# Two-level first-layer products in the last two groups of a fused attention and Fourier-mix kernel

## The chip, the cores and the metric

The kernel runs on one core of a Trainium2 chip. The core has engines that run side by side, each through its own list of instructions in order: TensorE (PE) multiplies matrices into eight banks of PSUM, VectorE (DVE) does elementwise work, ScalarE (ACT) applies functions and copies, GpSimd (POOL) does elementwise work on SBUF alone, and SyncE (SP) issues DMA transfers. They wait for each other through semaphores. The metric is the device time of one execution in microseconds (us), lower is better; the median of the runs shown is compared.

## The reference

All arrays are float32. There are 8 batches, 8 heads, 576 rows and a head dimension of 64, so that a row has 512 values after the heads are joined.

```python
q_s = softmax of q over its last axis
k_s = softmax of k over the sequence
x   = q_s @ (k_s^T v), heads joined               # (8, 576, 512)
mixed = real(fft over the columns of fft over the rows of x)
u   = x + mixed
un  = (u - mean(u)) / sqrt(var(u) + 1e-6)         # over the last axis
out = u + relu(un @ w_ch1) @ w_ch2                # w_ch1 512 x 2048, w_ch2 2048 x 512
```

## The kernel before, in words

The 8 x 576 rows are worked on as nine groups of 512 rows: eight groups of a batch's own rows, and one, number 8 in the code, that collects the 64 rows left over in every batch ("shared"). The groups run in the order 0 to 6, 8, 7. A group's place in that list is its `order`, so that order 7 is the shared group and order 8 is the last one. Attention, the Fourier mixing and the normalization of the following group run between the matrix products of the current one; in the last two orders only the normalization of the last group is left to run beside them, in the down half of order 7.

The two layers are most of the work. Each is a product of a 2 x 2 block matrix of weights with a 2 x 2 block matrix of activations, done with Winograd's form of Strassen's scheme: seven products (numbered 1 to 7, in the order 1, 6, 5, 7, 2, 4, 3 of `ORDER`) in the place of eight, and some sums of blocks before and after.

The up half (`up`, L1532) makes h = relu(un @ w_ch1). It goes through four quarters j. A quarter takes two pairs of column blocks of w_ch1 (i = 0, 1) and for each of the seven products runs four matmuls of 256 columns, L1544: two row blocks of the contraction for each i. `strassen` (L1499) places the products in three PSUM banks: 1 and then 2 in `ba`, 6, 7 and 4 in `bb`, 5 and 3 in `bc`, each added onto what is there. Between them ACT copies product 1 out (s1, L1515), DVE forms u2 and u3 (L1514) and the four blocks of h (L1555), and ACT applies relu (L1551, L1556). As an example, h22 is u3 plus product 5, and h12 is u2 plus products 5 and 3. At the end of the quarter `a_side` (L405 to L408) makes the four block sums of h that the second layer's products need, on DVE in orders 7 and 8 and on POOL before.

The down half (`deep_down`) makes h @ w_ch2 and adds it to u. There the products are already done at two levels: product 1 is done at one level (L1641), the others are split again into seven products of 128-column matmuls (L1671), two first-level products beside each other as a unit. `a_step` (L1617) makes the sums of h for them, `ends` (L1678 and the copies at L1685 and L1692) takes the results out of the banks, `into` (L1621) and `sums` (L1624) add the results to the rows x of the group, on POOL up to order 6 and on DVE in orders 7 and 8.

The normalization (`norm`) lays the normalized rows out as `unT`, seven blocks of 512 values per partition: four raw ones and the three or four block sums that the first layer needs (L1396, L1400, L1405).

The weights don't fit beside the activations. All block sums of the weights are made once, early on, and written to DRAM: `w1s` for the first layer at one level, `w2s` and `w2d` for the second at one and two levels. A list, `plan`, holds the stream of weight blocks of all orders. Four buffers hold it: when the block n has served its last product, `used(n)` issues the load of block n + 4 on SP's queue. SP issues its transfers in order.

The order of the work is written out by hand: every step has a time in a list, `timed` adds the steps of one order, and the list sorted by these times is recorded; each engine then runs its own instructions in that recorded order. The times have no other meaning. `UP` is the length of an up half in this list and `TWICE` that of a down half.

Of the kernel before, what the change touches and what calls it, by code (L numbers as in the profile page):

```python
# [52 lines left out]
HD = D // 2  # L53
# [66 lines left out]
def at(t, script):  # L120
    return [(t + dt, step) for dt, step in script]
# [17 lines left out]
class _Block:  # L139
    def __init__(self, ctx, tc, q, kT, v, w1, w2, ft, cd, out):  # L140
# [3 lines left out]
        nc = self.nc  # L144
# [6 lines left out]
        c = self.const  # L151
# [30 lines left out]
        nc.gpsimd.memset(self.sign[:], -1.0)  # L182
        nc.gpsimd.memset(self.sign[0:W], 1.0)
        d = self.dram
        self.w1s = [d.tile([P, 7, HD], F32, tag=f"w1s{p}", name=f"w1s{p}", bufs=1) for p in range(NP)]
        self.w2s = d.tile([7, P, NP, HD], F32, tag="w2s", name="w2s", bufs=1)

        self.w2d = d.tile([P, len(DEEP), GT], F32, tag="w2d", name="w2d", bufs=1)
        self.plan, self.base = [], {}
        for at in range(1, B + 1):  # L190
            self.base[at] = len(self.plan)
            self.plan += [self.w1s[p][:].rearrange("p a n -> p (a n)") for pair in PAIRS for p in pair]
# [59 lines left out]
    def flat(self):  # L252
        return self.turned().rearrange("p r n -> p (r n)")
# [163 lines left out]
    def combine(self, layer, p):  # L417

        nc = self.nc
        w = self.w2sb if layer else self.w1sb  # L420

        pairs = lambda a: a.rearrange("p (s n) -> p s n", s=2)
        temp = lambda n: self.work.tile([P, 2, HD], F32, tag=n, name=n, bufs=1)[:]
        if layer == 0 and p < 2:
            t, four = [temp("s1"), temp("u2")] if p == 0 else [temp("u3"), temp("s1")], None
        else:
            a = p // 2 * 2 - 2 + NP * (p % 2) if layer == 0 else NP + 2 * (p % 2)
            four = self.w1sb[:, a:a + 2, :].rearrange("p a n -> p (a n)")
            if layer and p % 4 == 3:
                four = self.spare_words  # L430
            t = [pairs(four[:, i * D:(i + 1) * D]) for i in range(2)]
            if layer and p % 4 == 2:
                t, four = [temp("s1"), temp("u2")], None
        quarter = lambda i: w[:, p + NP * (i // 2), (i % 2) * HD:(i % 2 + 1) * HD]
        place = lambda i: t[i > 4][:, int(i in (4, 6)), :]
        halves = lambda a: a.rearrange("p (s n) -> p s n", s=2)
        if layer == 0:
            ops = ((4, ALU.add, 2, 3), (2, ALU.subtract, 0, 2), (5, ALU.subtract, 4, 0), (6, ALU.subtract, 1, 5))
            engines, times = (nc.vector,) * 4, (0, 0.4, 0.8, 1.2)
            to, first, second = self.w1s[p][:], slice(0, 2), slice(2, 3)  # L440
# [1091 lines left out]
    def up(self, order, g):  # L1532

        nc, V = self.nc, self.nc.vector
        steps = []
        base, e = self.base[order], V if order >= B - 1 else nc.gpsimd
        for j in range(NP // 2):
            hp = lambda i, h=self.hpairs(j, 2): h[:, :, i, :]

# [22 lines left out]
            job = self.strassen(product, 1, {(1, 1): c11, (2, 1): other(1), (2, 2): other(3), (1, 2): other(2)})  # L1562
            t = 2 * len(ORDER) * j
            steps += at(t, job) + [(t + 2 * len(ORDER) - 0.5 + 5 * i * (j < NP // 2 - 1), lambda n=base + 2 * j + i: self.used(n)) for i in range(2)]
        return steps

    def used(self, n):
# [23 lines left out]
    def deep_down(self, g, order):  # L1591
# [24 lines left out]
            to = own(m)  # L1616
            e.tensor_tensor(out=to(o), in0=to(x), in1=to(y), op=op)  # L1617

        def into(u, d, m):
            x = self.xs[g, u][:, :, d * HD:(d + 1) * HD].rearrange("p c (e n) -> p c e n", n=P)  # L1620
            E.tensor_tensor(out=x, in0=x, in1=tile(m), op=ALU.add)  # L1621

# [57 lines left out]
        def ends(unit, n):  # L1680
# [14 lines left out]
            if n == 3:  # L1695
# [1 line left out]

        after = {(2, 4): [(7, into, 1, 0, 4), (9, into, 0, 0, 2)],
                 (7, 6): [(1, sums, 6, 1), (3, into, 0, 1, 6), (5, sums, 7, 6), *(((7, into, 1, 0, 7), (9, into, 1, 1, 7)) if last else ())],
                 (5, 3): [(0.6, into, 1, 1, 5), (1.2, into, 0, 1, 5), (1.8, into, 0, 1, 3)] if last else  # L1700
                         [(4, into, 1, 0, 7), (5.5, into, 1, 1, 7), (7, into, 1, 1, 5), (8.5, into, 0, 1, 5), (10, into, 0, 1, 3)]}
        names = {1: ("bb", "bb"), 2: ("bc", "bb"), 4: ("ba", "bb")}
        n, t = 2 * len(ORDER), 0
# [130 lines left out]
def kernel(ctx: ExitStack, tc: tile.TileContext, q, kT, v, w1, w2, ft,  # L1834
                                                           cd, out):
    blk = _Block(ctx, tc, q, kT, v, w1, w2, ft, cd, out)

    def timed(t, order, g):
        b = order + 1
# [91 lines left out]
    t = 0  # L1931
    for order, g in enumerate(groups[1:], 1):
        later += timed(t, order, g)
        t += UP + (TWICE if order > 1 else UP)
# [59 lines left out]
```

## Time and profile before

| what | value |
|---|---|
| three runs | 1006.04, 1007.01 and 1007.47 us; median 1007.01 us |
| span of the profiled execution | 1006.6 us, the only time shown of that execution; 0.4 us below the median of the runs |
| up half of order 7 | 815.03 to 863.51 us |
| down half of order 7 | 863.51 to 908.37 us |
| up half of order 8 | 908.37 to 956.72 us |
| down half of order 8, to the last product | 956.72 to about 1002.6 us |

The limits of the halves are the starts of PE's matmuls of L1544 and L1641 in the time line. In the time line a row is a start, a length, the engine, the line, the operation, output and inputs, the shape and the number of records; in brackets stand the idle time before it and what ended it. PE's ends are modelled and overlap the next start, so that the pace of PE is read from start to start. A row of the groups view ends with busy time, the mean of one in ns, and the idle time before such instructions. A row of the stretches view has the length, the busy time of PE, PE's weight loads (PEld), DVE, ACT and POOL with their counts, the granted TensorE clock, the busy share of the DMA engines and GB/s. A DMA row has the size of one transfer and the median time from issue to landing.

### The profile page before, as it was taken

How to read it: one execution, taken by the hardware profiler on the slowest of the kernel's cores; microseconds unless marked ns; L12 is line 12 of the kernel's file. 1: busy time of each engine (PE TensorE's matmuls, PEld its weight loads, DVE VectorE, ACT ScalarE, POOL GpSimd, SP SyncE). 2: the span in 40 equal slices, each digit the busy share in tenths (PEclk: the TensorE clock that was granted, in tenths of full speed). 3: DMA queues.
4: the chain of work that ended last, by engine and by line, in shares of the span. 5: the costliest groups of instructions: out<-in, count | busy, mean ns of one | idle time of the engine just before them, and what ended most of it. 6: DMA issues, size and time to landing. Idle time of an engine off the chain costs nothing.

```text
span 1006.6 us, 19808 instructions
## 1 busy us (share of the span) xinstructions
PE 995.6 (99%) x7562; PEld 855.7 (85%) x7562; DVE 718.6 (71%) x1356; ACT 493.2 (49%) x1277; POOL 442.9 (44%) x445
## 2 busy tenths in 40 slices
PE   8999999999999999999999999999999999999998
PEld 6844464888888899889988998899889998998897
DVE  6898898666765887588756877688667945685563
ACT  4585642872468228832775177625772342151200
POOL 4263420357535637664655465655646450040000
PEclk9999999999999999999999999999999999999999
DMA  9987499687989666975677577847753765674573
GB/s 300 258 281 245 158 240 346 205 243 226 342 283 272 230 230 219 266 237 210 251 220 242 206 269 237 253 174 270 231 204 135 267 213 200 224 265 172 183 256 132
DMA packets 123559, 236.37 MB, mean 235 GB/s; under 512 B 24184, under 2 KB 88440, under 8 KB 112840
## 3 DMA queue, kind: packets, MB, share of 16 engines
q1 hardware_dynamic: 123096, 234.58, 71.0%
q8 instruction: 60, 0.98, 0.4%
q14 instruction: 35, 0.29, 0.1%
q10 hardware_dynamic: 288, 0.26, 0.1%
q0 software_dynamic: 80, 0.26, 0.1%
HBM read 199.94 MB, written 39.06 MB: 237 GB/s over the span
## 4 chain that ended last, share of the span: by engine, by line
PE 87%; DVE 7%; ACT 3%; DMA 1%; issue 1%; SPq 0%; POOL 0%; DVEq 0%; POOLq 0%
PE bb L1544 16%; PE ba L1544 11%; PE bc L1544 11%; PE bb L1671 10%; PE ba L1671 7%; PE bc L1671 7%; PE bb L1641 5%; PE bc L1479 2%; PE bb L1760 2%; PE two L840 2%; PE one L755 2%; PE two L1207 1%; PE two L1264 1%; PE ba L1479 1%; PE bc L1760 1%; PE ba L1760 1%
## 5 line engine op out<-in xcount | busy, mean ns | idle before, releaser
L1544 PE MATMUL bb<-unT,big 128*128 128x256 f32 x768 | 183.3, 380 | 0.0
L1544 PEld LDWEIGHTS bb<-unT,big 128*128 128x128 f32 x768 | 144.8, 190 | 20.7 <-DVE u L1514 0.7
L1556 ACT ACTIVATE big<-big 128x512 f32<-128x512 f32 x96 | 59.8, 629 | 147.6 <-DVE big L1555 141.0
L1544 PE MATMUL ba<-unT,big 128*128 128x256 f32 x512 | 123.9, 382 | 0.0
L1544 PE MATMUL bc<-unT,big 128*128 128x256 f32 x512 | 121.5, 380 | 0.1
L817 ACT ACTIVATE qT<-q 32x128 f32<-32x128 f32 x384 | 117.9, 307 | 5.9 <-DVE q L807 0.8
L1544 PEld LDWEIGHTS bc<-unT,big 128*128 128x128 f32 x512 | 96.9, 190 | 13.7 <-DVE big L1555 0.5
L1544 PEld LDWEIGHTS ba<-unT,big 128*128 128x128 f32 x512 | 95.5, 190 | 13.9 <-issue 0.5
L1514 DVE TENSOR_TENSOR u<-bb,s 128x512 f32<-128x512 f32 x66 | 45.2, 685 | 85.0 <-PE bb L1544 66.5
L1671 PE MATMUL bb<-big 128*128 128x128 f32 x848 | 103.8, 276 | 0.2 <-DVE u L1678 0.2
L1671 PEld LDWEIGHTS bb<-big 128*128 128x128 f32 x848 | 98.9, 192 | 1.0 <-DVE u L1678 1.0
L1390 POOL COPY unT<-unT 32x256 f32<-32x256 f32 x98 | 42.0, 428 | 90.2 <-DVE unT L1382 85.9
L1621 POOL TENSOR_TENSOR x<-x,big 128x512 f32<-128x512 f32 x45 | 60.9, 1368 | 46.0 <-DVE big L1678 19.7
L1617 DVE TENSOR_TENSOR big<-big 128x512 f32<-128x512 f32 x98 | 79.9, 842 | 0.0
L1671 PE MATMUL ba<-big 128*128 128x128 f32 x640 | 79.0, 276 | 0.0
L1671 PEld LDWEIGHTS ba<-big 128*128 128x128 f32 x640 | 75.0, 192 | 0.8
L1390 ACT COPY unT<-unT 32x256 f32<-32x256 f32 x126 | 50.7, 402 | 31.3 <-DVE unT L1382 29.5
L804 POOL TENSOR_TENSOR q<-q,qm 128x512 f32<-128x512 f32 x24 | 25.8, 1073 | 88.2 <-DVE qm L799 53.1
L405 POOL TENSOR_TENSOR big<-big 128x512 f32<-128x512 f32 x24 | 30.4, 1268 | 68.4 <-ACT big L1556 68.4
L1641 PE MATMUL bb<-big 128*128 128x256 f32 x256 | 58.3, 379 | 0.0
L1555 DVE TENSOR_TENSOR big<-bc,u 128x512 f32<-128x512 f32 x64 | 44.0, 688 | 17.3 <-PE bc L1544 16.4
L1641 PEld LDWEIGHTS bb<-big 128*128 128x128 f32 x256 | 48.0, 190 | 6.1
(336 smaller groups left out, 1917.9 us busy)
## 6 DMA issues: line engine op xcount, KB each, us to landing
big<-w2d SPq DMA_DIRECT2D x67, 1024.0 KB, 4.6
big<-w1s SPq DMA_DIRECT2D x64, 896.0 KB, 4.7
big<-w2s SPq DMA_DIRECT2D x16, 1024.0 KB, 4.8
big<-in_w_dram SPq DMA_DIRECT2D x21, 512.0 KB, 6.0
w2d<-big SPq DMA_DIRECT2D x42, 256.0 KB, 6.5
kb<-in_kT_dram SPq DMA_DIRECT2D x28, 320.0 KB, 7.8
q<-in_q_dram SPq DMA_DIRECT2D x28, 256.0 KB, 6.0
vt<-in_v_dram SPq DMA_DIRECT2D x84, 80.0 KB, 2.7
```

Source lines behind the costliest of these rows:

```text
L405: e1.tensor_tensor(out=to(4), in0=at(2), in1=at(3), op=ALU.add)
L817: nc.scalar.activation(to[t, i * Q:i * Q + Q], one, ACT.Exp)
L1390: copy(to, of)
L1514: plus = lambda t: V.tensor_tensor(out=temp(t), in0=box["bb"][:], in1=box["s1"][:], op=ALU.add)
L1544: nc.tensor.matmul(bank()[:, i, :], lhsT=w[:, WA_AT[m], k * P:(k + 1) * P], rhs=self.unT[g][:, B_AT[m], k, :], start=first and i == 0 and ...
L1555: steps = [(0, lambda: V.tensor_tensor(out=hp(i), in0=bank()[:], in1=u()[:], op=ALU.add)), (0.8, lambda: nc.scalar.activation(hp(i), hp(i) ...
L1556: (0.8, lambda: nc.scalar.activation(hp(i), hp(i), ACT.Relu))]
L1617: e.tensor_tensor(out=to(o), in0=to(x), in1=to(y), op=op)
L1621: E.tensor_tensor(out=x, in0=x, in1=tile(m), op=ALU.add)
L1641: nc.tensor.matmul(box[name][:, i, :], lhsT=h[p][:, A_AT[m], i * P:(i + 1) * P], rhs=self.stream[n][:, p, :], start=p == 0 and (m != 1 or ...
L1671: nc.tensor.matmul(box[place[n]][:, i, :], lhsT=own(m)(A_AT[n])[:, f, :], rhs=w[:, r // 2, r % 2 * P:r % 2 * P + P], start=first and f == ...
L1760: nc.tensor.matmul(bank()[:, i, :], lhsT=h[p][:, A_AT[m], i * P:(i + 1) * P], rhs=w[:, p, :], start=first and i == 0 and p == 0, stop=p == ...
```

## The change

In orders 7 and 8 the function `wide_up` takes the place of `up`. Products 2 and 4 of order 7, and 2, 3 and 4 of order 8 (`WIDE`), leave the four quarters and are done each for all four quarters at once, at two levels, as a unit of seven products with four 128-column matmuls (`wide_unit`). The units stand behind the first quarter. The quarters keep the products 1, 6, 7, 5 and, in order 7, 3.

- Banks: in a quarter product 7 now has the bank `one` to itself, 1 has `ba`, 6 has `bb`, 5 and 3 share `bc`. In a unit 1 and 2 share `ba`, 6 and 4 use `bb`, 5 and 3 share `bc`, 7 has `one`.
- Results: a unit leaves its product in a slot of h that the a-side sums will fill later (`WIDE_AT`: slots 5, 6 and 4 for products 2, 3 and 4). `more` on POOL joins it with the other parts of h, in the first quarter after the unit, in the later ones ahead of the quarter's own sum where that can be (h12 in order 8) or after it (h21). h11 is a DVE sum of product 1's bank and the slot.
- Sums of h: of the four block sums of a quarter, two stay on DVE and two go to POOL, and all stand in the next quarter's sequence; the last quarter has all four on DVE.
- Operands: the raw weight blocks of products 2, 4 and 3 are loaded once, during the down half of order 6, into buffers that have no further use (`wide_load`: kb; vt, q and qT; F and ft). Their block sums are made by `wide_sums`: product 2's on DVE in the down half of order 6, those of 4 and 3 on POOL in the up half of order 7. The block sums of `unT` for each unit are made on POOL in order 7 and on DVE in order 8, 128x128 each.
- Five `into` steps at the end of order 7's down half go from DVE to POOL.
- The weight stream is the same. The eight DRAM tiles `w1s` become one, `w1c`, with the same contents.

```diff
+SHORT = (1, 6, 7, 5)
+UNIT, WIDE_AT = 7.2, {2: 5, 3: 6, 4: 4}
+WIDE = {B - 1: (2, 4), B: (2, 3, 4)}
...
-        self.w1s = [d.tile([P, 7, HD], F32, tag=f"w1s{p}", name=f"w1s{p}", bufs=1) for p in range(NP)]
+        self.w1c = d.tile([P, NP, 7, HD], F32, tag="w1s", name="w1s", bufs=1)
+        self.w1s = [self.w1c[:, p] for p in range(NP)]
...
-        base, e = self.base[order], V if order >= B - 1 else nc.gpsimd
+        base, e = self.base[order], nc.gpsimd
+        if order >= B - 1:
+            return self.wide_up(order, g)
...
+    def wide_load(self, m):
+        self.wide[m], pairs = self.wide_places(m)
+        for i, t in enumerate(pairs):
+            p = NP // 2 * (1 - i)
+            raw = self.w1c[:, p:p + NP // 2, WA_AT[m], :]
+            if t is not None:
+                self.nc.sync.dma_start(t, raw)
+                continue
+            for k in range(2):
+                self.nc.sync.dma_start(self.wide[m][2 * i + k], raw[:, :, k * P:(k + 1) * P])
...
+    def wide_unit(self, g, m, e, *at_sums):
...
+        place = {1: "ba", 2: "ba", 6: "bb", 4: "bb", 5: "bc", 3: "bc", 7: "one"}
...
+            for j in range(4):
+                nc.tensor.matmul(box[name][:, j, :], lhsT=self.wide[m][A_AT[n]][:, j, :], rhs=b_at(B_AT[n]),
+                                 start=first and j == 0, stop=True, skip_group_check=True)
...
+        def ends(n):
+            if n == 1:
+                nc.scalar.copy(temp("s1"), box["ba"])
+            if n == 6:
+                plus(temp("u2"), "bb", "s1")
+            if n == 7:
+                plus(temp("u3"), "one", "u2")
+                plus(to(3), "bc", "u3")
+            if n == 2:
+                nc.scalar.copy(to(0), box["ba"])
+            if n == 4:
+                plus(to(2), "bb", "u3")
+            if n == 3:
+                plus(to(1), "bc", "u2")
...
+        for k, n in enumerate(ORDER):
+            steps += [(1.02 * k, lambda n=n: product(n)), (1.02 * k + 0.9, lambda n=n: ends(n))]
...
+    def wide_up(self, order, g):
+        base, wide = self.base[order], WIDE[order]
+        products = [m for m in (*SHORT, 3) if m not in wide]
+        size = 2 * len(products)
+        def part(t, j, done):
+            def product(m, i):
+                name = {1: "ba", 6: "bb", 7: "one", 5: "bc", 3: "bc"}[m]
...
+                for k in range(2):
+                    nc.tensor.matmul(box[name][:, i, :], lhsT=w[:, WA_AT[m], k * P:(k + 1) * P], rhs=self.unT[g][:, B_AT[m], k, :],
+                                     start=m != 3 and i == 0 and k == 0, stop=k == 1, skip_group_check=True)
...
+            for k, m in enumerate(products):
+                for i in range(2):
+                    put(2 * k + i, product, m, i)
...
+            put(3.9, lambda: plus(temp("u2"), "bb", own(0) if j == 0 else got("s1")))
+            put(5.9, lambda: plus(temp("u3") if j else hp(1), "one", got("u2")))
+            put(7.9, lambda: plus(hp(3), "bc", got("u3") if j else own(1)))
...
+            if 3 not in wide or j == 0:
+                put(size + 0.7 * (3 in wide) - 0.1, lambda: plus(hp(2), "bc", got("u2")))
+            else:
+                put(4.7, lambda: more(WIDE_AT[3], got("u2"), 3))
+                put(8.7, lambda: plus(hp(2), "bc", own(WIDE_AT[3])))
...
+            put(1.95, lambda: plus(hp(0), "ba", own(WIDE_AT[2])))
+            put(6.7, lambda: more(1, got("u3"), 4))
+            if last:
+                sides(size + 2.6, size + 3.4, True)
+            else:
+                sides(size + (3.95 if 3 in wide else 2.3), size + (8.3 if 3 in wide else 3), False)
...
+        if order == B - 2:
+            steps += [(t + UP + dt, lambda m=m: blk.wide_load(m)) for m, dt in ((2, 4), (4, 12), (3, 25))]
+            steps += at(t + UP, blk.wide_sums(2, blk.nc.vector, 40, 41, 44, 45))
+        if order == B - 1:
+            steps += at(t, blk.wide_sums(4, blk.nc.gpsimd, 10.5, 10.6, 10.7, 10.8) + blk.wide_sums(3, blk.nc.gpsimd, 33, 34.6, 43, 44.6))
```

More of the change, by code (lines that the diff above doesn't have):

```diff
@@ L191, in __init__ @@
             self.base[at] = len(self.plan)
-            self.plan += [self.w1s[p][:].rearrange("p a n -> p (a n)") for pair in PAIRS for p in pair]
+            self.plan += [self.w1s[p].rearrange("p a n -> p (a n)") for pair in PAIRS for p in pair]
             one = lambda m: self.w2s[WB_AT[m]].rearrange("p a n -> p (a n)")
@@ L439, in combine @@
             engines, times = (nc.vector,) * 4, (0, 0.4, 0.8, 1.2)
-            to, first, second = self.w1s[p][:], slice(0, 2), slice(2, 3)
+            to, first, second = self.w1s[p], slice(0, 2), slice(2, 3)
             one, two = halves(w[:, p, :]), quarter(3).unsqueeze(1)
@@ L1564, in up, with wide_places @@
             steps += at(t, job) + [(t + 2 * len(ORDER) - 0.5 + 5 * i * (j < NP // 2 - 1), lambda n=base + 2 * j + i: self.used(n)) for i in range(2)]
+        return steps
+    def wide_places(self, m):
+        flat = lambda t, pattern: t[:].rearrange(pattern)
+        cut = lambda t, *at: [t[:, i:i + GT] for i in at]
+        new = lambda n, k: [self.work.tile([P, D], F32, tag=n, name=n, bufs=3)[:] for _ in range(k)]
+        if m == 2:
+            kb = flat(self.kb, "p r g s -> p (r g s)")
+            pairs, some = [kb[:, 0:2 * GT], kb[:, 2 * GT:4 * GT]], [*cut(kb, 4 * GT), *new("q", 2)]
+        elif m == 3:
+            F = flat(self.F, "p r n -> p (r n)")
+            pairs, some = [F[:, 0:2 * GT], self.ft[:, 0:2 * GT]], [*cut(F, 2 * GT), *cut(self.cd, 0), *cut(flat(self.ZT, "p k n -> p (k n)"), 0)]
+        else:
+            vt = flat(self.vt, "p c n -> p (c n)")
+            pairs, some = [vt[:, 0:2 * GT], None], [*new("qT", 2), *cut(flat(self.T, "p r i t -> p (r i t)"), 0)]
+        rows = lambda t: t.rearrange("p (j n) -> p j n", j=NP // 2)
+        w = {4 + i: rows(t) for i, t in enumerate(some)}
+        for i, t in enumerate(pairs):
+            for k in range(2):
+                w[2 * i + k] = rows(t)[:, :, k * P:(k + 1) * P] if t is not None else rows(new(("q", "qT")[k], 1)[0])
+        return w, [t if t is None else rows(t) for t in pairs]
@@ new lines, in wide_load, with wide_sums, make @@
+    def wide_load(self, m):
+        self.wide[m], pairs = self.wide_places(m)
+        for i, t in enumerate(pairs):
+            p = NP // 2 * (1 - i)
[5 more added lines that the diff above has]
+                self.nc.sync.dma_start(self.wide[m][2 * i + k], raw[:, :, k * P:(k + 1) * P])
+    def wide_sums(self, m, e, *times):
+        def make(o, x, y, op):
+            w = self.wide[m]
+            e.tensor_tensor(out=w[o], in0=w[x], in1=w[y], op=op)
+        some = (4, 2, 3, ALU.add), (5, 4, 0, ALU.subtract), (2, 0, 2, ALU.subtract), (6, 1, 5, ALU.subtract)
+        return [(t, lambda a=a: make(*a)) for t, a in zip(times, some)]
@@ L1699, in deep_down @@
                  (7, 6): [(1, sums, 6, 1), (3, into, 0, 1, 6), (5, sums, 7, 6), *(((7, into, 1, 0, 7), (9, into, 1, 1, 7)) if last else ())],
-                 (5, 3): [(0.6, into, 1, 1, 5), (1.2, into, 0, 1, 5), (1.8, into, 0, 1, 3)] if last else
+                 (5, 3): [(4, into, 1, 0, 7, G), (5.5, into, 1, 1, 7, G), (7, into, 1, 1, 5, G), (8.5, into, 0, 1, 5, G), (10, into, 0, 1, 3, G)] if E is V and not last else
+                         [(0.6, into, 1, 1, 5), (1.2, into, 0, 1, 5), (1.8, into, 0, 1, 3)] if last else
                          [(4, into, 1, 0, 7), (5.5, into, 1, 1, 7), (7, into, 1, 1, 5), (8.5, into, 0, 1, 5), (10, into, 0, 1, 3)]}
@@ L1933 @@
         later += timed(t, order, g)
-        t += UP + (TWICE if order > 1 else UP)
+        t += ups(order) + (TWICE if order > 1 else UP)
     steps += [(before + scale * t, step) for t, step in later]
```

92 lines of the change are left out of this document (90 added, 2 removed).

## The prediction

> **What bounds the kernel now.** I read the page first, then stretches of the last two groups, then the time lines of TensorE (PE) and VectorE (DVE) in them. "Order 7" and "order 8" are these groups; each has an up half and a down half.
>
> ```profile
> span 1006.6 us, 19808 instructions
> PE 995.6 (99%) x7562; PEld 855.7 (85%) x7562; DVE 718.6 (71%) x1356; ACT 493.2 (49%) x1277; POOL 442.9 (44%) x445
> ...
> PEclk9999999999999999999999999999999999999999
> ...
> PE 87%; DVE 7%; ACT 3%; DMA 1%; issue 1%; SPq 0%; POOL 0%; DVEq 0%; POOLq 0%
> ```
>
> PE is busy in 99% of the span and carries 87% of the chain that ended last. So a change pays by giving PE less work, and costs wherever PE has to wait. The two up halves that change are these stretches (columns: us, busy us of PE, PEld, DVE, ACT, POOL, clock, DMA share, GB/s):
>
> ```profile
> 815.03:863.51 48.48, 48.48 (x227) 42.48 (x226) 23.05 (x34) 11.24 (x19) 6.48 (x5) 1.00 0.53 185
> ...
> 908.37:956.72 48.35, 48.35 (x227) 42.55 (x226) 24.51 (x37) 11.21 (x19) 0.00 (x0) 1.00 0.49 174
> ```
>
> PE never pauses in them; DVE is busy in half of them, ACT in a quarter, POOL next to never. PE's own time line gives the prices (start, us; the profile counts two records for each matmul instruction):
>
> ```profile
> 815.03 1.89 PE L1544 MATMUL ba<-unT,big 128*128 128x256 f32 x8
> 816.76 1.89 PE L1544 MATMUL bb<-unT,big 128*128 128x256 f32 x8
> 818.49 1.89 PE L1544 MATMUL bc<-unT,big 128*128 128x256 f32 x8
> 820.22 1.89 PE L1544 MATMUL bb<-unT,big 128*128 128x256 f32 x8
> 821.94 1.89 PE L1544 MATMUL ba<-unT,big 128*128 128x256 f32 x8
> ...
> 861.78 1.89 PE L1544 MATMUL bc<-unT,big 128*128 128x256 f32 x8
> 863.51 7.07 PE L1641 MATMUL bb<-big 128*128 128x256 f32 x32
> 870.41 1.95 PE L1671 MATMUL ba<-big 128*128 128x128 f32 x16
> 872.20 1.95 PE L1671 MATMUL bb<-big,unT 128*128 128x128 f32 x16
> ...
> 890.07 1.95 PE L1671 MATMUL ba<-big 128*128 128x128 f32 x16
> 892.19 2.05 PE L1671 MATMUL bb<-big 128*128 128x128 f32 x16 [0.17 <-DVE u L1678]
> 894.08 1.95 PE L1671 MATMUL bc<-big 128*128 128x128 f32 x16
> ```
>
> Start to start, four 256-column instructions take 1.73 us (815.03 to 816.76), sixteen 6.90 (863.51 to 870.41), and eight 128-column ones 1.79 (870.41 to 872.20), so one of these takes 0.2235.
>
> **The change, part by part: the products.** One first-layer product over a whole group is 16 instructions of 256 columns, 6.90 us. At two levels it is 7 products of 4 instructions of 128 columns: 28 x 0.2235 = 6.26. The deep down half already runs this shape at this pace, with weight loads as frequent. Five products (two in order 7, three in order 8) give 5 x 0.64 = 3.2 us of PE time back.
>
> **The new sequence.** Before, a quarter ran the products 1, 6, 5, 7, 2, 4, 3, and DVE took product 5 out of bank bc while 2 and 4 ran; then 3 was added onto bc. In order 7 the short list is 1, 6, 7, 5, 3. Product 3 is added onto the bank that 5 has just filled, and h22, the sum of 5 with u3, must be read out of it in between, since it may not contain 3. The recorded order says the same: the first matmul of 3 waits for that DVE sum, and PE works in order. What such a wait costs follows from DVE's time line and the chain:
>
> ```profile
> 809.88 0.42 DVE L1678 TENSOR_TENSOR u<-bb,s 128x256 f32<-128x256 f32 x1 [2.14 <-PE bb L1671]
> ...
> 812.48 0.69 DVE L1396 TENSOR_TENSOR unT<-unT 128x512 f32<-128x512 f32 x1 [1.72 <-POOL unT L1390]
> 813.45 0.42 DVE L1678 TENSOR_TENSOR big<-bb,s 128x256 f32<-128x256 f32 x1 [0.28 <-PE bb L1671]
> ...
> 818.75 0.69 DVE L1514 TENSOR_TENSOR u<-bb,s 128x512 f32<-128x512 f32 x1 [2.45 <-PE bb L1544]
> 819.36 1.19 DVE L1405 TENSOR_TENSOR unT<-unT 128x512 f32<-128x512 f32 x1
> 822.14 0.69 DVE L1514 TENSOR_TENSOR u<-bb,s 128x512 f32<-128x512 f32 x1 [1.60 <-PE bb L1544]
> 822.87 0.69 DVE L1555 TENSOR_TENSOR big<-bc,u 128x512 f32<-128x512 f32 x1
> ```
>
> ```profile
> 891.80 0.34 DVE u L1678
> 892.14 0.04 issue
> 892.19 2.05 PE bb L1671 x16
> ```
>
> DVE starts 0.20 after a product's place in PE's queue is over (821.94 to 822.14) and reads a bank in 0.69. PE resumed 0.05 after DVE's end (892.14 to 892.19), and the product after a wait took 1.89 instead of 1.79 to the next start, 0.10 more. So each of order 7's four quarters loses 0.20 + 0.69 + 0.05 + 0.10 = 1.04 us: 4.15 us in all. Nothing can hide it, as PE has nothing to put between 5 and 3. Order 8 has 3 among its two-level products, so its quarters (1, 6, 7, 5) have no such wait.
>
> Is the lost time only its length? PE also waited early in the run:
>
> ```profile
> 42.70 1.97 PE L1467 MATMUL ba<-unT,big 128*128 128x256 f32 x8 [0.88 <-ACT eo L1326]
> 44.50 1.89 PE L1467 MATMUL bb<-unT,big 128*128 128x256 f32 x8
> ```
>
> After 0.88 us idle the eight records took 1.80 to the next start, near the usual 1.73, so the array kept its rate. By a rule it would not: the Trainium skill, "TensorE: Matmul & The Clock Gate", section "A second HAM failure mode: psum-queue depth-cycling", describes a kernel whose short pauses between groups on PSUM banks made the clock gate swing between half and full rate. By that rule the change would end far slower, and the last rival prices it from rows; the pause above speaks against it.
>
> **Inside the two-level units.** There the order is 1, 6, 5, 7, 2, 4, 3, at 0.89 each. After 7, DVE forms u3 (0.20 later, 0.73 to the next sum) and reads bc (0.69), and PE needs 0.05: 1.67 us, while products 2 and 4 cover 1.79. It fits by 0.12. I take 0; if DVE is 0.2 late in each of the five units, it costs about 0.5.
>
> **Sums.** The operand sums of the two-level unit on the weight side are four of 128x512 per product. Those of product 2 stand on DVE in order 6's down half, where DVE idles 2.14 before 809.88 and 1.72 before 812.48, against some 2.8 for four sums; the others, as the h-side joins, go to POOL.
>
> ```profile
> 813.25 1.27 POOL L1396 TENSOR_TENSOR unT<-unT 128x512 f32<-128x512 f32 x1 [0.81 <-DVE unT L1396]
> 814.48 7.19 POOL L1621 TENSOR_TENSOR x<-x,big 128x512 f32<-128x512 f32 x5
> ```
>
> ```profile
> L1020 POOL TENSOR_TENSOR T<-F 128x128 f32<-128x128 f32 x1 | 0.5, 461 | 0.0
> ```
>
> In order 7 POOL now has, from 814.5: eight 128x128 sums (3.7 us by the 461 ns row), the five additions to x (7.2), and product 4's four weight sums (5.1 at 1.27). The second of these last is needed by product 6 of unit 4, some 16.8 us into the half; it is done 3.7 + 7.2 + 2.5 = 13.4 us after 814.5, so 12.9 into it. Without these 3.9 us PE would wait there, once. In order 8 a quarter gives POOL two joins and two a-side sums, 4 x 1.27 = 5.1 of 6.9 us; DVE's read of bc for h12 waits for a join, but bc is wanted again only three products (5.2 us) later. DVE loses the five additions to x and two of four a-side sums in three quarters. A side sum on DVE with both operands in SBUF took 1.19 instead of 0.69 beside POOL (819.36), a sum from a bank 0.69 (818.75); so the reads PE waits for are not stretched. All this I take as 0, with up to 1 us for both halves if DVE falls behind; a gain is excluded, since PE waits for none of it now.
>
> **Scalar engine.** Per quarter a fifth pass of 0.63 at most (next row) in 7 to 9 us: hidden.
>
> ```profile
> L1556 ACT ACTIVATE big<-big 128x512 f32<-128x512 f32 x96 | 59.8, 629 | 147.6 <-DVE big L1555 141.0
> ```
>
> **Transfers.** Seven new loads, 3 MB in pieces of 1 KB or less, stand on SP's queue among order 6's down-half weights. None waits for anything unfinished, so SP isn't blocked; but weight loads queue behind them.
>
> ```profile
> big<-w2d SPq DMA_DIRECT2D x67, 1024.0 KB, 4.6
> big<-w1s SPq DMA_DIRECT2D x64, 896.0 KB, 4.7
> ...
> big<-in_w_dram SPq DMA_DIRECT2D x21, 512.0 KB, 6.0
> ```
>
> ```profile
> 790.00:800.00 10.00, 9.99 (x90) 9.80 (x88) 9.86 (x19) 3.48 (x5) 4.32 (x3) 1.00 0.83 297
> ```
>
> A weight block serves 16 instructions, 3.58 us; a load starts when its buffer is free and is wanted three blocks later, 10.7 us, against 4.6 to land: 6.1 spare. One more megabyte ahead of it takes 3.5 us at the 297 GB/s of the busiest stretch; by the row with the same 1 KB pieces (512 KB in 6.0) up to 12. I take the first, as the queue was fed continuously there: 0. By the other end, three times 5.9 late, less what later blocks catch up, 3 to 6 us. In order 8 a quarter of 6.9 us must cover a load of 4.7: 2.2 spare.
>
> Sum: -3.2 + 4.15 = +0.95 us on the 1006.6 us span, 1007.55. The median of the runs, 1007.01, is 0.4 above this span, so I expect 1007.9.
>
> **Rivals.** (a) Faster: the reads between 5 and 3 don't hold PE, and the 3.2 us arrive: 1003.8. No row of before has two products back to back on one bank with a read between, so only the argument from order stands against it; it would need less than 0.12 us lost at each place to pass 0.2%. (b) Slower: the 3 MB make order 6's weight stream late; the deciding point is a block landing over 10.7 us after its buffer is free: +4, 1011.9. DMA at 0.83 in 790 to 800 speaks for it, the 0.53 right after against it. (c) Slower: DVE or POOL runs late in the units and quarters, 0.2 or more at each of ten places: +2, 1009.9. (d) Each wait is followed by a product at half rate, 4 x 1.73 = 6.9 more: 1014.8.
>
> **Numbers.** Forecast 0.64, (a) 0.05, (b) 0.13, (c) 0.14, (d) 0.04. 0.2%, 2 us, is about what a measurement can tell from no change. The forecast's own range is 1006.6 to 1009.0: runs of before spread from 1006.04 to 1007.47, and the wait may be 0.9 to 1.2 four times. It lies within 0.2%; (a) is faster, (b), (c) and (d) slower. The range of all, 1006.4 to 1011.5, leaves out (a), (d) and the upper part of (b).
>
> **What would show it.** Right: in the profile after, order 7's up half about 2.9 us longer (51.3 for 48.5), with four PE waits of 0.8 to 1.0 on DVE's bc sum; order 8's about 46.4, without waits; order 6's down half unchanged. Wrong: no such waits; PE waits for DMA around 785 to 815; units slower than 6.26; waits on q, qT or T operands; a granted clock under 1.00.

## The result, and the profile after

The changed kernel takes 1008.79 us in the median of 11 runs (1007.75 to 1011.0), the kernel before beside it 1006.93 us in 11 runs (1005.67 to 1008.82). The ratio is 1.0018, with a 95% interval of 1.0009 to 1.0026: 1.86 us slower where 0.95 was forecast. That is under the 0.2% at which the prediction draws its line for a change. The interval reaches past that line, and its lower end lies above 1, so that the kernel is a little slower.

The page of the changed kernel, its first lines and the chain that ended last:

```profile
span 1006.7 us, 20192 instructions
PE 992.6 (99%) x7682; PEld 855.9 (85%) x7682; DVE 730.3 (73%) x1378; ACT 498.9 (50%) x1287; POOL 500.9 (50%) x492
...
PEclk9999999999999999999999999999999999999999
...
PE 88%; DVE 7%; ACT 2%; DMA 1%; issue 1%; SPq 0%; POOL 0%; DVEq 0%; POOLq 0%
```

PE is busy 3.0 us less than before (992.6 for 995.6), and yet the span is the same. Of the 3.0, 0.7 lies ahead of order 7, where PE's work is the same in both (808.16 and 807.44 us busy); from order 7's start on PE is busy 185.13 us for 187.41. Where the time went instead stands in the waits of PE from 810 to 960 us (us in total, times, the longest):

```profile
PE bc L1687 <- DVE big L1691: 3.5, 4, 1.1
PE bb L1874 <- DVE u L1881: 0.2, 1, 0.2
```

The first row is new, the second was there before. The two up halves, with the columns of the stretches shown in the prediction:

```profile
813.89:865.51 51.62, 48.16 (x274) 42.63 (x273) 25.62 (x37) 13.61 (x23) 36.59 (x33) 1.00 0.50 174
910.37:956.76 46.39, 46.39 (x298) 43.09 (x297) 30.36 (x51) 13.19 (x23) 20.14 (x15) 1.00 0.51 180
```

Order 7's half took 51.62 us for 48.48 before, with PE busy in 48.16 of them; order 8's took 46.39 for 48.35. Two of the four waits on PE's time line, the first and the second:

```profile
819.07 1.89 PE L1687 MATMUL bc<-unT,big 128*128 128x256 f32 x8
822.07 1.99 PE L1687 MATMUL bc<-unT,big 128*128 128x256 f32 x8 [1.11 <-DVE big L1691]
823.90 1.05 PE L1636 MATMUL ba<-unT,kb 128*128 128x128 f32 x8
...
841.64 1.89 PE L1687 MATMUL bc<-unT,big 128*128 128x256 f32 x8
844.31 1.99 PE L1687 MATMUL bc<-unT,big 128*128 128x256 f32 x8 [0.78 <-DVE big L1691]
846.14 1.89 PE L1687 MATMUL ba<-unT,big 128*128 128x256 f32 x8
```

They stand between product 5 and product 3, both in bank bc. Without a wait product 3 would start 1.73 after product 5. It starts 2.67 after it in the second quarter (841.64 to 844.31) and 3.00 in the first, so 0.94 and 1.27 are lost, and then the product itself takes 1.83 for 1.73 (844.31 to 846.14). The first wait is the longer one because of what VectorE had to do ahead of the read:

```profile
819.27 0.69 DVE L1691 TENSOR_TENSOR big<-one,u 128x512 f32<-128x512 f32 x1 [0.98 <-PE one L1687]
819.88 1.54 DVE L1410 TENSOR_TENSOR unT<-unT 128x512 f32<-128x512 f32 x1
821.34 0.68 DVE L1691 TENSOR_TENSOR big<-bc,big 128x512 f32<-128x512 f32 x1
```

The read of bc itself (821.34) takes the usual 0.68. The sum of unT in front of it has both operands in SBUF; POOL was adding to x just then, and it took 1.54. Product 5's place is over at 820.80 (819.07 and 1.73), so that by the prediction's 0.20 the read would have started at 821.00; it came 0.34 later.

From order 7's start to the end of the span the profile of before has 191.57 us (815.03 to 1006.6) and that of after 192.81 (813.89 to 1006.7): +1.24.

### The profile page after: what moved, and what is told of

Same layout as the page of the kernel before. It is cut to its first block, busy times and chain, and to the rows that moved or that the text cites. A ratio compares the mean times of both kernels' runs of the same rounds, so it can differ in the third digit from the quotient of the medians.

```text
span 1006.7 us, 20192 instructions
## 1 busy us (share of the span) xinstructions
PE 992.6 (99%) x7682; PEld 855.9 (85%) x7682; DVE 730.3 (73%) x1378; ACT 498.9 (50%) x1287; POOL 500.9 (50%) x492
## 4 chain that ended last, share of the span: by engine, by line
PE 88%; DVE 7%; ACT 2%; DMA 1%; issue 1%; SPq 0%; POOL 0%; DVEq 0%; POOLq 0%
PE bb L1551 12%; PE bb L1874 10%; PE ba L1551 8%; PE bc L1551 8%; PE ba L1874 7%; PE bc L1874 7%; PE bb L1844 5%; PE bc L1484 2%; PE bb L1964 2%; PE bc L1687 2%; PE two L845 2%; PE one L760 2%; PE two L1212 1%; PE two L1269 1%; PE ba L1484 1%; PE one L1687 1%
## 5 line engine op out<-in xcount | busy, mean ns | idle before, releaser
L1551 PE MATMUL bb<-unT,big 128*128 128x256 f32 x576 | 137.8, 381 | 0.0
L1551 PEld LDWEIGHTS bb<-unT,big 128*128 128x128 f32 x576 | 108.4, 190 | 15.6 <-DVE u L1519 0.6
L1551 PE MATMUL ba<-unT,big 128*128 128x256 f32 x384 | 93.7, 383 | 0.0
L1551 PE MATMUL bc<-unT,big 128*128 128x256 f32 x384 | 91.2, 380 | 0.1
L1563 ACT ACTIVATE big<-big 128x512 f32<-128x512 f32 x72 | 44.7, 628 | 77.9 <-DVE big L1562 71.3
L1551 PEld LDWEIGHTS bc<-unT,big 128*128 128x128 f32 x384 | 72.5, 190 | 10.5 <-DVE big L1562 0.5
L1519 DVE TENSOR_TENSOR u<-bb,s 128x512 f32<-128x512 f32 x50 | 34.2, 683 | 64.3 <-PE bb L1551 46.0
L1551 PEld LDWEIGHTS ba<-unT,big 128*128 128x128 f32 x384 | 71.3, 190 | 10.6 <-issue 0.5
L410 POOL TENSOR_TENSOR big<-big 128x512 f32<-128x512 f32 x24 | 30.5, 1270 | 67.6 <-ACT big L1563 67.6
L1874 PE MATMUL bc<-big 128*128 128x128 f32 x416 | 50.7, 275 | 0.0
```

The source lines that it names most:

```text
L410: e1.tensor_tensor(out=to(4), in0=at(2), in1=at(3), op=ALU.add)
L1519: plus = lambda t: V.tensor_tensor(out=temp(t), in0=box["bb"][:], in1=box["s1"][:], op=ALU.add)
L1551: nc.tensor.matmul(bank()[:, i, :], lhsT=w[:, WA_AT[m], k * P:(k + 1) * P], rhs=self.unT[g][:, B_AT[m], k, :], start=first and i == 0 and ...
L1563: (0.8, lambda: nc.scalar.activation(hp(i), hp(i), ACT.Relu))]
L1874: nc.tensor.matmul(box[place[n]][:, i, :], lhsT=own(m)(A_AT[n])[:, f, :], rhs=w[:, r // 2, r % 2 * P:r % 2 * P + P], start=first and f == ...
```

## The experiments

The times of before were taken beside each kernel's, on the same chip.

| kernel | order 7's up half, us | median, us (runs) | before, us | ratio, 95% interval |
|---|---|---|---|---|
| changed | 51.62 | 1008.79 (11) | 1006.93 | 1.0018, 1.0009 to 1.0026 |
| own bank for product 3 | 47.10 | 1004.14 (11) | 1006.82 | 0.9976, 0.9967 to 0.9985 |
| units in order 8 only | 53.55 | 1009.46 (6) | 1006.82 | 1.0026, 1.0014 to 1.0038 |
| units in order 7 only | 51.60 | 1010.53 (5) | 1006.82 | 1.0040, 1.0026 to 1.0053 |
| no units, loads and sums left | 53.55 | 1011.59 (5) | 1006.82 | 1.0048, 1.0034 to 1.0062 |
| the same without POOL's weight sums | 48.48 | 1007.29 (10) | 1007.41 | 0.9999, 0.9989 to 1.0008 |
| two reads of bc | 54.50 | 1012.06 (4) | 1007.41 | 1.0045, 1.0029 to 1.0060 |
| four reads of bc | 65.25 | 1022.65 (4) | 1007.41 | 1.0148, 1.0132 to 1.0164 |
| three units in order 7 too | 54.48 | 1012.15 (5) | 1007.41 | 1.0044, 1.0030 to 1.0058 |
| the same, rearranged | 46.99 | 1006.32 (11) | 1007.15 | 0.9987, 0.9978 to 0.9996 |

**The read between 5 and 3: a bank of its own.** Product 3 of order 7's quarters goes to a free bank, and h12 is made in two sums:

```diff
-                name = {1: "ba", 6: "bb", 7: "one", 5: "bc", 3: "bc"}[m]
+                name = {1: "ba", 6: "bb", 7: "one", 5: "bc", 3: "two"}[m]
...
-                put(size + 0.7 * (3 in wide) - 0.1, lambda: plus(hp(2), "bc", got("u2")))
+                put(8.6, lambda: plus(hp(2), "bc", got("u2")))
+            if 3 not in wide:
+                put(size - 0.1, lambda: plus(hp(2), "two", own(2)))
```

> Edit: in order 7 product 3 goes to a bank of its own (one of the 'two' banks), so that nothing in the bank of product 5 has to be read out ahead of it; DVE gets one more sum of 0.69 us per quarter (h12 is made in two steps). Theory (the four waits of PE on DVE's read of bc are the whole loss): the four PE waits on the bc sum vanish, order 7's up half takes 48.48 - 1.3 = 47.2 us instead of 51.6, and the time is 4.4 us under the changed kernel's, about 1004.4, 2.5 under before. Rival (the loss is spread over the sums on DVE and POOL, the waits only show where it surfaces): PE waits elsewhere in the half instead, which stays over 49 us; the time stays above 1006.

Measured: 1004.14 us, 2.7 us faster than before and 4.6 faster than the changed kernel. The stretches of its up halves:

```profile
813.23:860.33 47.10, 47.10 (x275) 43.02 (x273) 28.00 (x41) 12.74 (x22) 36.60 (x33) 1.00 0.55 191
905.20:951.59 46.39, 46.39 (x299) 43.12 (x298) 30.36 (x51) 13.18 (x23) 20.13 (x15) 1.00 0.50 180
```

PE is busy in all of order 7's half, which is 4.52 us shorter than in the changed kernel although VectorE has four sums more (41 for 37). So the four waits cost 4.5 us, and all else that the change adds costs next to nothing there. This version beats both kernels. By the medians of the spans, 1001.9 for 1005.05, it is 3.15 below before, which is the 3.2 that the five units were to give; the runs gain 0.45 less, and where that lies is told at the end of this section.

**Reading the bank longer.** The sum h22 of order 7's quarters is made two or four times over, with the same result:

```diff
-            put(7.9, lambda: plus(hp(3), "bc", got("u3") if j else own(1)))
+            for r in range(2 if 3 not in wide else 1):
+                put(7.9 + 0.01 * r, lambda: plus(hp(3), "bc", got("u3") if j else own(1)))
```

> The changed kernel with the sum h22 of order 7's quarters made twice, so that VectorE reads bank bc twice before product 3 may be added to it. Theory (PE waits for the end of that read, and the pause costs its length): 0.69 more four times, 2.8 in all: 1011.5, PE waits of 1.4 to 1.8, clock 1.00. Rival (the clock drops to half after a pause of this length): 1.7 more after each, 1018.

> The same with the sum made four times. Pauses of about 2.9, the first 3.2. Length alone: 4 x 3 x 0.69 = 8.3 more than the changed kernel, 1017.1. If the clock drops to half after a pause of about 3 us as it did after 3.25 in the kernel with neither order at two levels, up to 1.7 more after each: 1018.8 if after the first alone, 1023.9 if after all four.

With two reads the half takes 54.50 us, 2.88 more than with one for the 2.8 expected, and the difference from before grows from 1.86 us to 4.65; the waits are these, and the clock stays at 1.00:

```profile
PE bc L1687 <- DVE big L1691: 6.3, 4, 1.8
```

With four reads the waits come to 12.2, which is 8.7 more than with one, but the half is 13.6 longer (65.25). Two waits of the same length show why, on PE's time line and in the stretches from each product's start to the next:

```profile
850.56 1.99 PE L1687 MATMUL bc<-unT,big 128*128 128x256 f32 x8 [2.96 <-DVE big L1691]
852.39 1.89 PE L1687 MATMUL ba<-unT,big 128*128 128x256 f32 x8
...
862.42 3.68 PE L1687 MATMUL bc<-unT,big 128*128 128x256 f32 x8 [2.96 <-DVE big L1691]
865.92 1.90 PE L1687 MATMUL ba<-unT,big 128*128 128x256 f32 x8
```

```profile
850.56:852.39 1.83, 1.83 (x8) 1.62 (x9) 0.00 (x0) 0.61 (x1) 0.81 (x1) 1.00 0.00 0
862.42:865.92 3.50, 3.50 (x8) 2.76 (x9) 0.00 (x0) 0.61 (x1) 0.74 (x1) 0.52 0.19 28
```

After one pause of 2.96 the product takes 1.83 at a granted clock of 1.00, after the next one 3.50 at 0.52. The product after the fourth wait, also 2.96, takes 3.40, and the one after the first, 3.29, is slow too (3.12 at 0.58). So three of four such pauses were followed by half the clock for some 3 us, and one was not; the pauses of 0.8 to 1.8 in the kernels with one and two reads never were, and between 1.8 and 2.96 none was seen. The median, 1022.65, lies between the two cases that were expected, 1018.8 for one fall of the clock and 1023.9 for four. The Trainium skill, "TensorE: Matmul & The Clock Gate", section "What's actually happening", says that the array falls to half rate after an idle window of about 3.4 us, and that this window runs freely, so that the point of change varies. The trace agrees that equal pauses can end either way, and has the drop after less: 2.96 us of idle time.

**Which order gives what: one order alone.** In the one kernel order 7's up half, in the other order 8's, is the old `up`, and in a third one both are. The loads, the weight sums and the additions on POOL stay as in the changed kernel. The edit for units in order 8 alone:

```diff
-        if order >= B - 1:
+        if order >= B:
             return self.wide_up(order, g)
```

> Edit: order 7's up half is that of the kernel before (one level, sums on DVE); order 8's is the changed one; loads and weight sums all stay. Theory of the waits: order 8 has none, so this is 1.9 us under before, about 1005.0; order 7's up half 48.5, order 8's 46.4. Rival (the loads and sums that stay cost something in order 6 or 7): less than 1 us under before, or no gain.

> Edit: order 8's up half is that of the kernel before, order 7's is the changed one; loads and sums stay. Theory of the waits: -1.3 from two units and +4.4 from four waits (1.27 + 3 x 0.94 as the trace shows them, and 0.1 each for the product after), so 3.0 us over before, about 1009.9. Rival (the loss of the whole change does not sit in order 7): within 1 us of before.

Order 7 alone came out where it was expected (1010.53 for 1009.9), with an up half like the changed kernel's (51.60). Order 8 alone did not: 1009.46 for 1005.0. Its order 8 takes 46.39, as it should, but its order 7, with no unit in it, takes 53.55. The kernel with neither shows the same:

> Edit: both up halves are those of the kernel before; the seven loads in order 6's down half, the weight sums on DVE and POOL and the five additions on POOL stay, and nothing uses the loaded blocks. Theory of the waits: all of this is hidden, so the time is that of before, 1006.9, within 0.5. Rival (the loads or sums delay PE in orders 6 and 7): 0.6 us or more over before; 0.6 is what the changed kernel lost beyond the 1.24 us that its trace shows from order 7's start to the end.

It lost 4.8 us although no product is changed. So the theory that the moved sums and loads cost nothing was wrong as stated, and the rival held. Its time lines of PE, of VectorE and of POOL:

```profile
829.89 1.89 PE L1551 MATMUL bc<-unT,big 128*128 128x256 f32 x8
835.03 3.63 PE L1551 MATMUL bb<-unT,big 128*128 128x256 f32 x8 [3.25 <-DVE u L1519]
838.46 1.98 PE L1551 MATMUL ba<-unT,big 128*128 128x256 f32 x8
```

```profile
828.16 1.20 DVE L410 TENSOR_TENSOR big<-big 128x512 f32<-128x512 f32 x1 [0.77 <-ACT big L1563]
829.39 1.64 DVE L411 TENSOR_TENSOR big<-big 128x512 f32<-128x512 f32 x1
830.96 1.75 DVE L412 TENSOR_TENSOR big<-big 128x512 f32<-128x512 f32 x1
832.81 1.57 DVE L413 TENSOR_TENSOR big<-big 128x512 f32<-128x512 f32 x1
834.30 0.68 DVE L1519 TENSOR_TENSOR u<-bb,s 128x512 f32<-128x512 f32 x1
```

```profile
827.54 1.27 POOL L1611 TENSOR_TENSOR F<-ft 128x512 f32<-128x512 f32 x1
828.89 1.60 POOL L1611 TENSOR_TENSOR cd<-F 128x512 f32<-128x512 f32 x1
830.45 1.71 POOL L1611 TENSOR_TENSOR ft<-F,ft 128x512 f32<-128x512 f32 x1
832.12 1.71 POOL L1611 TENSOR_TENSOR ZT<-F,cd 128x512 f32<-128x512 f32 x1
```

In the old half the four sums of h (L410 to L413) stand on VectorE directly ahead of the sum that empties bank bb. POOL now makes the weight sums of product 3 at that moment, and both engines slow down: VectorE needs 6.1 us (828.16 to 834.30) for sums that take 2.7 without POOL beside them, and PE waits 3.25 for the bank. The product after it takes 3.43 at half clock. Start to start that is 3.41 and 1.70 too much, 5.1 in all, as the half shows (53.55 for 48.48). Of the six executions of the kernel with order 8 alone, the two at a mean clock of 1.000 took 1007.64 and 1008.30 us, the four at 0.997 or 0.998 1009.44 to 1010.79: so the same pause may well have lowered the clock in some and not in others, which only a profile of each would show. To test the cause, POOL's weight sums alone were left out:

```diff
-            steps += at(t, blk.wide_sums(4, blk.nc.gpsimd, 10.5, 10.6, 10.7, 10.8) + blk.wide_sums(3, blk.nc.gpsimd, 33, 34.6, 43, 44.6))
```

> The kernel with neither order at two levels, which lost 4.8 us, without the eight weight sums of products 4 and 3 on GpSimd in order 7's up half (nothing uses them there); the loads, the sums of product 2 and the five additions on POOL stay. Theory: its 3.25 us wait and the half clock after it came from these sums alone, which stretched the four block sums of h that VectorE had to make ahead of the read for PE; without them the time is that of the kernel before, 1006.8 within 0.7, and the block sums take 0.69 each. Rival (the 3 MB of loads or the additions on POOL are to blame for part): 1008.5 or more.

```profile
813.67:862.15 48.48, 48.48 (x227) 42.48 (x226) 23.52 (x34) 11.24 (x19) 8.06 (x6) 1.00 0.53 186
```

The half is 48.48 again, the sums take 0.69 each, and the time is that of before (ratio 0.9999). So the loads, the additions on POOL and product 2's sums on VectorE in order 6 cost nothing that can be measured; the weight sums cost 5 us in this kernel. In the changed one they cost PE no wait of this kind. There two of the four sums of h are on POOL and all stand later, in the next quarter, and POOL itself comes to product 3's weight sums only from 844.68 us on, with the joins between them. No run tells which of the two differences it is.

**Three units in order 7 too.** Product 3 leaves order 7's quarters as well, which takes the reads between 5 and 3 away and saves a unit more:

```diff
-WIDE = {B - 1: (2, 4), B: (2, 3, 4)}
+WIDE = {B - 1: (2, 4, 3), B: (2, 3, 4)}
...
-            e, times = (V, (-5.2, -5.1, -3.1, -3.0) if k else (-3.05, -3, -1.3, -1.2)) if order == B else (
+            e, times = (V, (-5.2, -5.1, -3.1, -3.0) if k else (-3.05, -3, -1.3, -1.2)) if order == B or k == 2 else (
...
-... blk.wide_sums(3, blk.nc.gpsimd, 33, 34.6, 43, 44.6))
+... blk.wide_sums(3, blk.nc.gpsimd, 10.9, 11, 11.1, 11.2))
```

> Order 7 also gets product 3 as a two-level unit, so that its quarters are 1, 6, 7, 5 as in order 8; product 3's weight sums on POOL follow those of product 4 at once, its sums of unT go to DVE. Theory (the read of bank bc between 5 and 3 is what costs, a unit saves 0.64): no wait of a quarter is left and one unit more is saved, so 0.6 below the kernel with the own bank: 1003.5. Rival (GpSimd, with eight weight sums in a row, is late for the third unit and the joins behind it): PE waits for POOL in order 7's up half, 2 us or more, 1005.5 or above.

The rival came in: 1012.15. In this kernel one block of h, in order 7's last quarter, is read ahead of its relu, so it does not compute the reference; in its trace that relu waits for the read, after all that is shown here. PE's waits in order 7's up half:

```profile
PE ba L1636 <- ACT big L1656: 3.6, 1, 3.6
PE bc L1636 <- DVE big L1645: 0.6, 1, 0.6
```

With eight weight sums in a row POOL came to the first join of h only at 835.69. ScalarE stood at the relu that waits for it, and behind that relu, in its queue, stood the copy that empties bank ba: 3.6 us of PE, and half clock after it, for longer than above: four products took 6.60 us (838.18 to 844.78) at a clock of 0.53, 3.0 more than at full clock. The second wait is VectorE's, and shows what the two engines do to each other at its plainest (VectorE's time line, then POOL's):

```profile
831.95 0.68 DVE L1645 TENSOR_TENSOR u<-one,u 128x512 f32<-128x512 f32 x1
...
833.27 1.33 DVE L1627 TENSOR_TENSOR big<-unT 128x128 f32<-128x128 f32 x1
834.53 1.34 DVE L1627 TENSOR_TENSOR big<-unT,big 128x128 f32<-128x128 f32 x1
```

```profile
831.96 1.27 POOL L1611 TENSOR_TENSOR cd<-F 128x512 f32<-128x512 f32 x1
833.18 1.27 POOL L1611 TENSOR_TENSOR ft<-F,ft 128x512 f32<-128x512 f32 x1
834.41 1.31 POOL L1611 TENSOR_TENSOR ZT<-F,cd 128x512 f32<-128x512 f32 x1
```

A 128x128 sum on VectorE that takes 0.28 in order 8, where POOL is idle, ends 0.15 after the POOL instruction that it met. Had they shared evenly it would have taken 0.56, so it seems to have waited. The sum at 831.95, with one operand in a bank, keeps its 0.68 beside the same kind of POOL instruction. The Trainium skill, "SBUF — State Buffer", section "Who interferes with whom", says that a VectorE instruction with two SBUF inputs and a GpSimd one that reads SBUF exclude each other from a shared port, and that the one that comes second is blocked. These rows agree. The rows of the kernel with neither agree only in part: there, with both engines at such sums back to back, one of each is done per 1.64 us (829.39 to 834.30 for three), less than the 1.96 that 0.69 and 1.27 make one after the other.

The kernel was then rearranged: the first quarter's relu passes behind the last unit, the third unit's unT sums earlier, and product 4's sums of h ahead of product 2's in the down half:

```diff
-                put(done[m] - t + 1.6, relu, i)
+                put(max(done.values()) - t + (1.6 if done[m] == max(done.values()) else 0.1), relu, i)
...
-            e, times = (V, (-5.2, -5.1, -3.1, -3.0) if k else ...
+            e, times = (V, (-20.5, -20.4, -7.3, -7.25) if k == 2 and order < B else (-5.2, -5.1, -3.1, -3.0) if k else ...
...
-                    put(early + step * k + j * 1.1 + 0.3 + late * (i == 2), a_step, m, o)
+                    put(early + step * k + (1.1 * (1 - j) + 0.9 if E is V and not last and i == 1 else 1.1 * j + 0.3) + late * (i == 2), a_step, m, o)
```

> Three units in both orders again, with the three causes of the last such kernel's waits taken away: the relu passes of the first quarter stand behind the last unit on ScalarE, the third unit's sums of unT are made early on VectorE (two in the first quarter, two between the units), and the down half of order 7 makes product 4's sums of h ahead of product 2's. Theory (six units save 0.64 each, no wait is left): 0.6 below the kernel with the own bank, about 0.3% below the kernel before of its call. Rival (VectorE and GpSimd hold each other up in order 7's up half wherever both read SBUF): PE waits of 0.3 to 1 in the units, a second of gain gone, level with the kernel with the own bank or above it by 1.

Measured: 0.8 us below before (0.9987), and so short of the own bank's 2.7. The long wait is gone. The stretches of order 7's two halves:

```profile
815.05:862.04 46.99, 46.95 (x299) 43.34 (x298) 32.17 (x45) 12.98 (x23) 37.80 (x34) 1.00 0.55 192
...
862.04:908.44 46.40, 45.18 (x369) 43.82 (x368) 38.30 (x70) 17.92 (x37) 17.40 (x20) 1.00 0.76 260
```

Order 7's up half is only 0.11 shorter than with the own bank, where 0.64 was expected: its three units take 19.36 us (821.96 to 841.32), where three of 6.26 make 18.78. Its down half takes 46.40 where that of the changed kernel takes 44.86. There VectorE, which still has the last quarter's sums to make, is late (PE's waits from 810 to 960 us):

```profile
PE bb L1874 <- DVE u L1881: 0.8, 2, 0.6
PE bb L1874 <- DVE unT L1820: 0.4, 1, 0.4
```

The rival is right that the sixth unit doesn't pay. The two halves together lose 1.4 us against the own bank. Set against before, the medians of the spans differ by 2.25 (0.9 below before for 3.15), so some 0.8 is not explained by them.

**The time outside the span.** The time of a run less its span is 2.19 to 2.32 us in all runs of the changed kernel, 1.72 to 1.89 in those of before. The kernels with the own bank and with two and four reads have 2.18 to 2.33, all others 1.73 to 1.89. Two kernels, with one run each, tested whether the length of the program does it, each the kernel before with idle instructions at the start of order 8:

```diff
+                    for _ in range(60):
+                        nc.tensor.matmul(t[0:1, 0:1], lhsT=self.sign[:], rhs=self.sign[:], start=True, stop=True, skip_group_check=True)
```

```diff
+                steps.append((0.1, lambda: [nc.gpsimd.memset(self.sign[:], 0.0) for _ in range(250)]))
```

> The kernel before with 60 one-element matmuls into an unused bank at the start of order 8. Looked at is the time of a run less its span: 1.73 to 1.89 in the runs of before and of the kernels with units in one order or none, 2.19 to 2.32 in the changed kernel and in the one with the own bank, whose PE program is the longest. If the length of PE's program makes the step, it is 2.2 or more here; if not, 1.8. The span itself grows by what the matmuls take, some us.

> The kernel before with 250 one-column memsets of a dead tile on GpSimd, which is idle there, in order 8: more instructions in all than the changed kernel has. If the step of 0.45 in the time outside the span comes with the length of the whole program, it is 2.2 or more here; if with PE's alone, 1.8. The span stays that of before.

They have 1.76 (1012.06 us at a span of 1010.3) and 1.73 (1008.03 at 1006.3). The first has as many PE instructions in its page as the changed kernel, 7682, so PE's length isn't it. The second was meant to have more in all than the changed kernel, but has 20058 for its 20192, so that by itself it settles little. The kernels with three units in both orders do: they have 7706 on PE, 20263 and 20267 in all, and 1.77 to 1.89. What makes these 0.45 us stays open.

## Why the prediction was right, point by point

**Products.** Right. Two units of order 7 take 12.56 us (823.90 to 836.46, the start of the next quarter), 6.28 each for 6.26 forecast. Order 8's half came out at 46.39 for 46.4. Inside a unit the read of bc fitted, as forecast: in unit 4 it ended at 835.34 on VectorE, 0.17 ahead of the product that needs it (835.51), where 0.12 was reckoned.

**The wait for bank bc.** Right in place, number and cause, and nearly in size: three times 0.94 and 0.10 as forecast, once 1.27 and 0.10. The four cost 4.5 us by the own bank's half, where 4.15 was the term. Mis-sized was the first: "so the reads PE waits for are not stretched" is true of the read (0.68), but the instruction ahead of it in VectorE's queue was stretched to 1.54. The row of before that shows this sum (819.36, 1.19) stands in the prediction; I used it for the side sums only, and didn't ask what stands behind it.

**The chance that the reads don't hold PE** (a) fell: they do, and by their length, as the two and four reads show. What it priced, 1003.8, is what the kernel without them takes (1004.14).

**Half rate after a wait** (d) fell for waits of this length: the granted clock is 1.00 in both halves and the product after a wait takes 1.83. The Trainium skill, "TensorE: Matmul & The Clock Gate", section "A second HAM failure mode: psum-queue depth-cycling", which was held against the change, speaks of short pauses without a length; here those of 0.8 to 1.8 us cost no rate, and those of about 3 us in the kernel with four reads mostly did. With reads four times as long (d) would have been a good part of the loss: some 4.9 of 13.6 us.

**Sums and joins** (c). Zero, as forecast, but for the first wait. In order 7 the second weight sum of product 4 ended on POOL at 828.24, 14.4 us into the half for 12.9 forecast, and PE wanted it at 831.05. But the reason given, that there is idle time enough on both engines, wasn't the whole one. The same weight sums in the kernel with neither order's units cost 5 us, by the stretched sums of h and the clock together. What runs on the two engines at the same moment mattered, and the working did not weigh that: in part the zero was luck.

**Transfers** (b). Zero, as forecast. The stretch from 790 to 800 us, with a DMA share of 0.83 and 297 GB/s before, now reads

```profile
790.00:800.00 10.00, 9.99 (x90) 9.80 (x89) 9.86 (x19) 3.77 (x6) 3.67 (x4) 1.00 0.96 360
```

so the queues moved 360 GB/s where I had reckoned with 297, and PE waited for no weights. Order 6's down half takes 52.37 us (761.52 to 813.89) for 52.36 before (762.67 to 815.03). The kernel without POOL's weight sums, which keeps the loads, confirms it in the time.

**The sum.** Forecast +0.95; with the 0.33 by which the first wait is longer, 1.28, for +1.24 in the profiles. The medians differ by 1.86 (0.9 to 2.6 by the interval). Of the 0.62 between the two, 0.45 lies outside the span, in the step that no run explained; no row of before could have shown it. The step from the span to the median in the forecast, 0.4, set the span of one execution against the times of others: with 1.72 to 1.89 outside the span that execution took about 1008.4, 1.4 above the median. Nothing hung on it, as the forecast is 0.95 above the median either way.

## What to carry to other kernels

A read that has to come between two products in one bank cost PE 0.94 us and more each time here, the read and its latency, and nothing hid it, so such a product was worth a bank of its own even at the price of one more sum. Before work is moved to GpSimd, look at which VectorE instructions with two SBUF operands run beside it, and what is queued behind those: in the cases here the stretched instruction was not the one that PE waited for, but stood ahead of it. And a pause of TensorE cost little more than its length up to 1.8 us; most of those of 2.96 to 3.3 cost about 1.7 more, and one of 3.6 cost 3.0 more.

## What the runs showed that was not expected

- Equal pauses of 2.96 us were followed by full clock once and by half clock twice in one execution (1.83, 3.50 and 3.40 us for the same product).
- VectorE's 128x128 sum with both operands in SBUF took 0.28 us alone and 1.33 beside GpSimd, as long as the GpSimd instruction, while sums from a bank kept their 0.69.
- The time outside the span has two values, 1.8 and 2.25 us, which belong to kernels and not to runs, and don't follow the length of the program.
